# One group of a fused attention and feed-forward kernel: the output store, one second-layer product and the key loads change places

## The chip, the cores and the metric

The kernel runs on one core of a Trainium2 chip. The time is device microseconds of one execution; the kernel before took 1843.82 us in the median of three runs (1843.07, 1843.82 and 1850.48). The engines are TensorE (PE for its matmuls, PEld for its weight loads), VectorE (DVE), ScalarE (ACT), GpSimd (POOL) and SyncE (SP), which here does nothing but issue DMAs.

## The reference

Two functions follow each other. First, attention against keys pooled 4 by 4, whose keys and values are the same matrix; then a feed-forward layer whose hidden units pass a softmax-weighted linear unit and a layer norm.

```
kv_pool = kv.reshape(B, H//4, 4, W//4, 4, C).mean(axis=(2, 4))      # B = 4, H x W = 384 x 32, C = 128
k = v = kv_pool.reshape(B, -1, C) @ w_sr                            # 768 keys in a batch
s = (q @ k.T) / sqrt(C);  a = exp(s - max(s));  a /= sum(a) + 1e-9  # 12288 queries in a batch
x = (a @ v).reshape(B * 12288, 128)
h = x @ w_in                                                        # 128 -> 1024
sm = exp(h - max(h)) / sum;   solu = h * sm
ln = (solu - mean) / sqrt(var + 1e-6) * g_ln
out = ln @ w_out                                                    # 1024 -> 128
```

## The kernel before, in words

The 4 x 12288 queries are cut into 384 tiles of 128 tokens (`NT`). Four tiles make a group (`GT = 4`, 96 groups), 24 groups a batch. Products are taken to nearly float32 precision by splitting each operand into a high and a low float16 part and adding three products.

A tile passes these steps, each named by its tensors in the profile:

- `s` (L587, PE): six matmuls of the queries with the 768 keys. DVE takes the maximum (`nm`, L608), ACT the exponential (L609) and the high half (`phl`, L611), DVE the low half (`phl`, L619). SP then issues a DMA transpose of `phl` into the group's tile `pT` (L622).
- `xa` (L647, PE): when all four tiles of a group lie in `pT`, 18 matmuls with 512 columns make the attention output for the whole group. They are handed out over four slots as 5, 5, 4 and 4. ACT and DVE take them out as `xh` (L654) and `xl` (L659).
- `zz` (L674, POOL) and `rz` (L682, DVE): the group's softmax sums and their reciprocals.
- `h` (L700, PE): six matmuls into the 1024 hidden units, with `junkd` (L708, DVE, the maximum), `e` (L724, ACT, the exponential), `u` (L738, DVE), `junk` (L803, ACT, the variance) and the two halves `uhl` (L755 and L762, POOL). SP issues a DMA transpose of `uhl` into `uT` (L777).
- `o` (L828, PE): 24 matmuls of 128 columns from `uT`, about three slots after its transpose was issued. Once in a group DVE scales the four tiles' result into `ob` (L851), and SP stores it (L860).

The order is written by hand. The main loop has a pass for each *slot*, one tile entering in each, and the tiles before it stand at later steps: in slot n, PE computes `s` of tile n+1, `h` of tile n-9 (`LH = 10`) and `o` of tile n-14 (`LO = 14`), and DVE, ACT, POOL and SP get their instructions in the same pass. Every engine runs its instructions in that order; semaphores join them. A group's slots are counted here from first to fourth by the remainder of the slot by 4 (0, 1, 2, 3). So the fourth slot of a group issues the last transpose into its `pT`, and the `xa` that needs all four begins two slots later, in the second slot of the next group.

PSUM has three buffers that `s` and `h` take in turn (`ps_r`): an `h` can begin only when DVE has read the `s` of that slot for its `phl` (L619).

The keys of the next batch are made beside all this. Each of the 16 parts of the next `kv` is loaded with one DMA of 384 KB (`kv_load`, L227) and added up by POOL in two halves (`kv_add`, L238, tensor `ka`). `kv_plan` gives the slots: the load in the first slot of a group, the two additions three and five slots behind the slot that it is reckoned from. In the kernel before, ACT issues 42 of these loads, in between its own work. SP issues the transposes of `phl` and `uhl` in every slot, the store in the third slot, and the load of the queries (`q_load`, L528) in the fourth.

Of the kernel before, what the change touches and what calls it, by code (L numbers as in the profile page):

```python
# [30 lines left out]
NT = B * TPB  # L31
GT = 4
GPB = TPB // GT
NG = NT // GT
# [9 lines left out]
LO = 14  # L44
# [17 lines left out]
FIT_AT = 302  # L62

SOON = {0: (), 1: (8, 8), 2: (8, 8), 3: (27, 33), 4: (39, 45), 5: (51, 54)}
LATE = {6: (12, 16, 18), 7: (16, 20, 22)}


@with_exitstack
def kernel(
# [15 lines left out]
    nc = tc.nc  # L85
# [61 lines left out]
    state = {}  # L147

    def kv_alloc(b):
        for n, w, dt, bufs in (  # L150
            ("kT", NK, F32, 1),
            ("ksq", NK, BF16, 1),
            ("kss", 2, F32, 4),
            ("vf", NK, F32, 1),
        ):
            state[n, b] = bat.tile([P, w], dt, tag=n, name=f"{n}_{b}", bufs=bufs)
        for n, w in (("knm", 3), ("sv", 2), ("bb", 5), ("kq", 3), ("dg", P)):
            state[n, b] = (
                state[n, 0]
                if 0 < b < B  # L160
                else bat.tile([P, w], F32, tag=n, name=f"{n}_{b}", bufs=1)
            )
        for n, dt, bufs in (
            (("kwh", F32R, 1), ("kwl", F32R, 1))
            if b == 0 or b >= B
            else (("kh", F16, 2), ("kl", F16, 2))
        ):
            state[n, b] = bat.tile([P, NK], dt, tag=n, name=f"{n}_{b}", bufs=bufs)
        vhl = dmt.tile([P, 2 * NKC, P], F16, tag="vhl", name=f"vhl_{b}")
        state["vhl", b] = vhl  # L170
        state["vh", b], state["vl", b] = vhl[:, :NKC, :], vhl[:, NKC:, :]
# [327 lines left out]
    def kv_plan(b):  # L499


        for pos in range(RR):


            if b == 1 and pos in SOON:
                for half, slot in enumerate(SOON[pos]):
                    yield slot, [partial(kv_add, b, half, pos)]
                continue
            slot = 6 * pos - (28 if b == 1 else 30)
            load, *adds = (slot // GT * GT, slot + 3, slot + 5)  # L510
            if b == 1 and pos in LATE:
                load, *adds = LATE[pos]
            yield load, [partial(kv_load, b, pos)]
            if pos:
                for half, add in enumerate(adds):
                    yield add, [partial(kv_add, b, half, pos)]
        for slot, half, *fs in key_steps(b):
            yield slot, [partial(f, b, half) for f in fs]
# [18 lines left out]
    def wide(g):  # L537
        return g < GPB or g >= NG

    def q_scale(g):  # L540
        if wide(g) or NG <= g:
            return
        qf = state["qf", g // QL][:, (g % QL) * 512 : (g % QL + 1) * 512]
        nc.gpsimd.tensor_scalar(
            qf, qf, state["kq", g // GPB][:, 1:2], 1.0, op0=ALU.mult, op1=ALU.mult
        )
# [80 lines left out]
    def values(g, qtr, part):  # L627
        share = {0: [0, 9, 9, 0], 1: [0, 6, 6, 6]}.get(
            g, [4, 5, 5, 4] if wide(g + 2) else [5, 5, 4, 4]
        )  # L630
        s0 = sum(share[:qtr])
        s1 = s0 + share[qtr]
        if s0 == s1:
            return
        cut = s0 + (s0 > 0 and (qtr > 1 or wide(g + 2)))
        s0, s1 = ((s0, cut), (cut, s1))[part]
        b = g * GT // TPB
        if s0 == 0 and s1:
            state["xa", g] = ps_x.tile([P, 512], F32, tag="x", name=f"xa_{g}")
        if s0 == s1:  # L640
            return
        xa, pT = state["xa", g], state["pT", g]
        vh, vl = state["vh", b], state["vl", b]
        seq = [(a, c, v) for c in range(NKC) for (a, v) in ((0, vh), (1, vh), (0, vl))]
        for n in range(s0, s1):
            a, c, v = seq[n]
            nc.tensor.matmul(  # L647
                xa, v[:, c, :], pT[:, :, a * NKC + c, :], start=n == 0, stop=n == len(seq) - 1
            )
# [195 lines left out]
        nc.gpsimd.tensor_tensor(f, f2, state.pop(("v3", g)), op=ALU.add)  # L845
        nc.gpsimd.tensor_tensor(f2, f, mhalf[:, :GT], op=ALU.pow)

    def final_out(g, to=None):
        _, f = state["f", g]
        ob = dmt.tile([P, GT, P], F32, tag="ob", name=f"ob_{g}")  # L850
        nc.vector.scalar_tensor_tensor(  # L851
            ob,
            state["po", g].rearrange("p (j c) -> p j c", j=GT),
            swi,
            f.unsqueeze(2).to_broadcast([P, GT, P]),
            op0=ALU.mult,
            op1=ALU.mult,
        )
        rows = out[g * GT * P : (g + 1) * GT * P, :] if to is None else to
        nc.sync.dma_start(rows.rearrange("(p j) c -> p (j c)", j=GT), ob.rearrange("p j c -> p (j c)"))  # L860

# [174 lines left out]
    def key_steps(b):  # L1036
        steps = [
            (70, 0, kv_kp, kv_ko), (71, 1, kv_kp, kv_ko), (74, 2, kv_kp, kv_ko),
            (72, 0, kv_sq), (75, 1, kv_sq),
            (77, 0, kv_kh), (79, 1, kv_kh),  # L1040
            (78, 0, kv_kl), (80, 1, kv_kl),
        ]
        if b < B - 1:
            return steps + [
                (82, 0, kv_vp, kv_vo), (83, 1, kv_vp, kv_vo), (86, 2, kv_vp, kv_vo),
                (84, 0, kv_v_high), (85, 0, kv_v_low), (87, 1, kv_v_high), (88, 1, kv_v_low),
            ]
        return steps + [
            (82, 0, kv_v_scale), (84, 1, kv_v_scale),
            (83, 0, kv_vt_high), (86, 1, kv_vt_high),  # L1050
            (86, 0, kv_vt_low), (88, 1, kv_vt_low),
            (90, 0, kv_v_turn),
        ]
# [3 lines left out]
    def at(t, fn, *args):  # L1057
        if 0 <= t < NT:
            fn(t, *args)

    def at_last(t, fn, *args):

        if 0 <= t < NT and t % GT == GT - 1:
            fn(t // GT, *args)

    def at_soon(t, fn):

        at_last(t, fn) if t >= GT else fn(0) if t == GT - 2 else None
# [9 lines left out]
    for slot in range(NT):  # L1078
        i = slot - LH
        av, qtr = divmod(slot - LAV - GT + 1, GT)  # L1080
        tb, ti = divmod(slot, TPB)
        if ti == 12 and tb + 1 < B:
            kv_alloc(tb + 1)
        qs = GT if slot < 2 * GT else 2 * GT + 1 if slot < 3 * GT else 3 * GT + QSP
        todo = plan.pop(slot, [])
        at(slot, scores_exp)
        for f in held:
            f()
        held = []
        if slot <= LH:  # L1090
            at(slot - 1, scores_split)
        at(i - 1, hidden_u)
        at_last(slot - XSP - 1, values_split)
        if slot < 9:
            for f in fill.pop(slot, []):
                f()
        if 0 <= av < NG:
            values(av, qtr, 0)
        if slot != 8:
            at(slot + 2 if slot < 8 else slot + 1, scores_pe)  # L1100
        at_soon(slot - NORM, values_norm)
        at_last(slot - FSC, final_scale)
        at(i - 1, hidden_high)
        at(i - 1, hidden_low)
        at_last(slot - FSC, final_root)
        if slot < NT and 0 < qs < slot and (slot - 1 - qs) % GT == 0:
            q_low(slot // GT + 1)
        if slot < NT and 0 < qs <= slot + 1 and (slot + 1 - qs) % GT == 0:
            q_scale((slot + 1) // GT + 1)
        if slot < NT - 1:  # L1110
            at(i - 1, hidden_var)
        at(i, hidden_max)
        at(i, hidden_exp)
        if slot == NT - 1:
            hidden_var(i - 1)
        for f in fill.get(slot, []):
            f()
        pairs = [st for st in todo if len(st) > 1 and st[0].func is not kv_add]
        for st in pairs:
            st[0]()  # L1120
        if 0 <= av < NG:
            values(av, qtr, 1)
        for st in pairs:
            held += st[1:]
        if slot >= LH:
            at(slot, scores_split)
        at_soon(slot - NORM, values_recip)
        at_soon(slot - NORM, values_recip_u)
        at(i + 1, hidden_pe)
        if slot < NT - 1:  # L1130
            at(slot - LO, final_pe)
        at(i - 1, hidden_turn)
        if slot % GT == GT - 1:
            q_load(slot // GT + 3)
        at_last(slot - LO - 1, final_out)
        at_last(slot - XSP, values_out)
        for st in todo:
            if st[0].func is kv_add:
                for f in st:
                    f()  # L1140
            elif len(st) == 1:
                st[0]()
        if slot < NT and 0 < qs <= slot and (slot - qs) % GT == 0:
            q_split(slot // GT + 1)
# [183 lines left out]
```

## Time and profile before

| | |
|---|---|
| median of three runs | 1843.82 us |
| the profiled execution | 1843.65 us |
| its span, first to last instruction | 1841.9 us |
| PE, DVE, ACT, POOL busy | 99%, 96%, 95%, 91% of the span |
| DMA transposes, `phl` and `uhl` | 384 and 383 |
| key loads issued by ACT and by SP | 42 and 22 |
| mean DMA rate over the span | 235 GB/s |

The share of busy time says little here, as four engines are nearly full. A wait between two of them and the time from one group to the next say more. The group's period is read as the time between the same instruction of two groups, here DVE's `u` (L738) of one tile in four.

### The profile page before, as it was taken

The numbers are of one execution on the slowest core, as the hardware profiler recorded it, in microseconds if no ns is written. First come the engines' busy times: TensorE is split into PE (matmuls) and PEld (weight loads), VectorE is DVE, ScalarE is ACT, GpSimd is POOL, SyncE is SP. The second block draws the span as 40 slices with busy tenths as digits, with TensorE's granted clock in tenths as the row PEclk, the third lists the DMA queues.
The fourth block names the chain that finished last, engine by engine and source line by source line (L and its number), as shares of the span: only waits on it lengthen the run. The fifth ranks groups of instructions, "written<-read, shape, count | busy, mean of one in ns | idle before, by whom it ended". The sixth has DMA issues, their size and how long they took to land.

```text
span 1841.9 us, 42770 instructions
## 1 busy us (share of the span) xinstructions
PE 1818.3 (99%) x15747; PEld 1218.5 (66%) x15747; DVE 1761.9 (96%) x2635; ACT 1742.6 (95%) x3129; POOL 1667.2 (91%) x1466
## 2 busy tenths in 40 slices
PE   8999999999999999999999999999999999999998
PEld 5577777777666666666666666666666666666666
DVE  6999999999999999999999998999999999999997
ACT  5999999999999999999999998999999999999997
POOL 5899999899999999989999998998988988888887
PEclk9999999999999999999999999999999999999999
DMA  9999999999999999999999999999999999999997
GB/s 301 203 249 230 230 253 232 247 230 237 242 241 241 246 245 242 246 235 235 247 239 241 242 222 230 247 239 224 222 233 230 232 235 231 220 235 224 230 223 168
DMA packets 1440027, 432.80 MB, mean 235 GB/s; under 512 B 1404608, under 2 KB 1408832, under 8 KB 1439552
## 3 DMA queue, kind: packets, MB, share of 16 engines
q1 hardware_dynamic: 1433616, 413.45, 112.6%
q10 hardware_dynamic: 6192, 16.52, 3.2%
q8 instruction: 126, 2.06, 0.5%
q14 instruction: 93, 0.76, 0.1%
HBM read 52.50 MB, written 25.17 MB: 42 GB/s over the span
## 4 chain that ended last, share of the span: by engine, by line
PE 46%; DVE 26%; ACT 15%; issue 9%; DMA 2%; POOL 1%; SPq 0%; DVEq 0%; ACTq 0%; POOLq 0%
PE o L828 13%; PE h L700 13%; PE s L587 10%; PE xa L647 10%; DVE junkd L708 8%; DVE phl L619 6%; DVE nm L608 5%; ACT e L724 4%; ACT junk L803 4%; DVE u L738 3%; ACT phl L611 3%; ACT s L609 2%; DVE ob L851 2%; DVE xl L659 2%; DMA kv<-in_kv_dram 1%
## 5 line engine op out<-in xcount | busy, mean ns | idle before, releaser
L762 POOL TENSOR_TENSOR uhl<-u,uhl 128x1024 f16<-128x1024 f32 x382 | 815.0, 2134 | 32.3 <-ACT uhl L753 0.6
L828 PEld LDWEIGHTS <-uT 128*128 128x128 f16 x9072 | 537.9, 98 | 89.1 <-issue 0.9
L828 PE MATMUL o<-wch,uT 128*128 128x128 f16 x6048 | 568.1, 219 | 0.1
L828 PE MATMUL o<-wcl,uT 128*128 128x128 f16 x3024 | 526.1, 219 | 0.0
L738 DVE SCALAR_TENSOR_TENSOR u<-h,rz,e 128x1024 f32<-128x1024 f32 x384 | 490.4, 1277 | 33.3 <-ACT e L724 32.7
L708 DVE TENSOR_SCALAR_CACHE_REDUCE junkd<-h,rz 128x1024 bf16<-128x1024 f32 x384 | 490.7, 1278 | 7.6 <-PE h L700 7.2
L647 PE MATMUL xa<-pT,vhl 128*128 128x512 f16 x1728 | 470.4, 380 | 5.4 <-DMA pT<-phl 5.4
L755 POOL TENSOR_SCALAR uhl<-u 128x1024 f16<-128x1024 f32 x379 | 395.8, 1044 | 83.9 <-DVE u L738 72.7
L724 ACT ACTIVATE e<-h,nm,rz 128x1024 f32<-128x1024 f32 x384 | 458.5, 1194 | 8.2 <-DVE junkd L708 8.2
L803 ACT ACTIVATE junk<-u,su 128x1024 bf16<-128x1024 f32 x384 | 438.0, 1141 | 0.1
L609 ACT ACTIVATE s<-s,nm 128x768 f32<-128x768 f32 x384 | 334.7, 872 | 47.6 <-DVE nm L608 47.1
L619 DVE SCALAR_TENSOR_TENSOR phl<-s,phl 128x768 f16<-128x768 f32 x384 | 365.8, 953 | 6.5 <-ACT phl L611 4.1
L608 DVE TENSOR_REDUCE nm<-s 128x1 f32<-128x768 f32 x384 | 360.1, 938 | 9.1 <-PE s L587 4.6
L611 ACT ACTIVATE phl<-s 128x768 f16<-128x768 f32 x384 | 311.1, 810 | 12.1
L700 PEld LDWEIGHTS <-xh 128*128 128x128 f16 x1536 | 144.0, 97 | 195.4 <-issue 27.1
L647 PEld LDWEIGHTS <-vhl 128*128 128x128 f16 x1728 | 162.4, 98 | 141.3 <-issue 16.0
L700 PE MATMUL h<-w_in_h,xh 128*128 128x512 f16 x768 | 228.9, 380 | 3.6 <-DVE rz L682 3.2
L700 PE MATMUL h<-w_in_l,xh 128*128 128x512 f16 x768 | 229.0, 380 | 0.0
L700 PE MATMUL h<-w_in_h,xl 128*128 128x512 f16 x768 | 228.8, 380 | 0.0
L587 PEld LDWEIGHTS <-qh 128*128 128x128 f16 x1152 | 122.6, 114 | 42.9
L587 PE MATMUL s<-kh,ql 128*128 128x384 f16 x576 | 140.8, 326 | 0.1
L587 PE MATMUL s<-kl,qh 128*128 128x384 f16 x576 | 140.8, 326 | 0.0
(153 smaller groups left out, 1820.4 us busy)
## 6 DMA issues: line engine op xcount, KB each, us to landing
qf<-in_q_dram SPq DMA_DIRECT2D x96, 256.0 KB, 3.8
out_dram<-ob SPq DMA_DIRECT2D x96, 256.0 KB, 2.9
kv<-in_kv_dram ACTq DMA_DIRECT2D x42, 384.0 KB, 4.3
kv<-in_kv_dram SPq DMA_DIRECT2D x22, 384.0 KB, 7.5
pT<-phl SPq DMA_TRANSPOSE x384, 4.0
uT<-uhl SPq DMA_TRANSPOSE x378, 4.6
raw_in<-in_moe_w_in_dram SPq DMA_DIRECT2D x1, 1024.0 KB, 5.1
raw_out<-in_moe_w_out_dram SPq DMA_DIRECT2D x1, 1024.0 KB, 9.6
```

Of the source, the lines that this page charges most:

```text
L587: nc.tensor.matmul(s[:, half, :384], tokens(lh)[:, j, :], rh[:, half * 384 : (half + 1) * 384], start=n == 0, stop=n == 2,)
L608: nc.vector.tensor_reduce(nm, s, axis=AX.XY, op=ALU.max, negate=True)
L619: nc.vector.scalar_tensor_tensor(phl[:, 1], state.pop(("s", t)), SC, phl[:, 0], op0=ALU.mult, op1=ALU.subtract)
L647: nc.tensor.matmul(xa, v[:, c, :], pT[:, :, a * NKC + c, :], start=n == 0, stop=n == len(seq) - 1)
L700: nc.tensor.matmul(h[:, hs], lh[:, ts], rh[:, hs], start=n == 0, stop=n == 2)
L708: nc.vector.tensor_scalar(junk, state["h", t], state["rz", g][1][:, j : j + 1], None, op0=ALU.mult, op1=ALU.min, accum_out=nm,)
L724: nc.scalar.activation(e, state["h", t], AF.Exp, bias=nm, scale=state["rz", g][0][:, js], accum_out=state["z2", g][:, js],)
L738: nc.vector.scalar_tensor_tensor(u, state.pop(("h", t)), state["rz", g][2][:, j : j + 1], state.pop(("e", t)), op0=ALU.mult, op1=ALU.mult, ...
L755: nc.gpsimd.tensor_scalar(uhl[:, 0, :], u, 1.0, 1.0, op0=ALU.mult, op1=ALU.mult)
L762: low.tensor_tensor(uhl[:, 1, :], u, uhl[:, 0, :], op=ALU.subtract)
L803: nc.scalar.activation(junk, u, AF.Square, scale=-float(DFF), bias=su, accum_out=state["v3", g][:, j : j + 1],)
L828: nc.tensor.matmul(po[:, ts], uT[:, a * NFC + c, :], w[:, c, :], start=start, stop=stop)
```

## The change

Three pieces of the order move; nothing is added or left out in the computation.

- *The store.* DVE's `ob` stays in the third slot, but its store is issued in the fourth, behind that slot's two transposes and ahead of the load of the queries.
- *The second slot's matmuls.* In the second slot of a group PE runs `o`, then `h`, then `xa`, where it ran `xa`, `h`, `o`.
- *The key loads.* The 42 loads that ACT issued are issued by SP, one slot later, in a group's second slot behind its two transposes. The additions keep their slots.

```diff
-LATE = {6: (12, 16, 18), 7: (16, 20, 22)}
+LATE = {6: (13, 16, 18), 7: (17, 20, 22)}
...
             slot = 6 * pos - (28 if b == 1 else 30)
-            load, *adds = (slot // GT * GT, slot + 3, slot + 5)
+            load, *adds = (slot // GT * GT + 1, slot + 3, slot + 5)
...
-            yield load, [partial(kv_load, b, pos)]
+            yield load, [partial(kv_load, b, pos, nc.sync)]
...
-    def final_out(g, to=None):
+    def final_out(g, to=None, later=False):
...
+        state["ob", g] = ob
+        if not later:
+            final_store(g, to)
+
+    def final_store(g, to=None):
+        ob = state.pop(("ob", g))
         rows = out[g * GT * P : (g + 1) * GT * P, :] if to is None else to
         nc.sync.dma_start(rows.rearrange("(p j) c -> p (j c)", j=GT), ob.rearrange("p j c -> p (j c)"))
...
-        if 0 <= av < NG:
+        o_first = slot % GT == 1
+        if o_first:
+            at(slot - LO, final_pe)
+        elif 0 <= av < NG:
             values(av, qtr, 1)
...
         at(i + 1, hidden_pe)
-        if slot < NT - 1:
+        if o_first:
+            if 0 <= av < NG:
+                values(av, qtr, 1)
+        elif slot < NT - 1:
             at(slot - LO, final_pe)
         at(i - 1, hidden_turn)
+        at_last(slot - LO - 2, final_store)
         if slot % GT == GT - 1:
             q_load(slot // GT + 3)
-        at_last(slot - LO - 1, final_out)
+        at_last(slot - LO - 1, partial(final_out, later=True))
```

SP's instructions from the second slot of a group to the first of the next, with a key load in the group. The first number behind a name is the tile's or the group's (`phl_193` is of tile 193, in slot 193; `ob_44` is of group 44). Before:

```order
L622 DMA_TRANSPOSE pT_48_13759<-phl_193_13803 128x12x128
L777 DMA_TRANSPOSE uT_182_13873<-uhl_182_13820 128x16x128
L622 DMA_TRANSPOSE pT_48_13759<-phl_194_13881 128x12x128
L777 DMA_TRANSPOSE uT_183_13943<-uhl_183_13893 128x16x128
L860 DMA out_0_dram<-ob_44_13945 128x512
L622 DMA_TRANSPOSE pT_48_13759<-phl_195_13951 128x12x128
L777 DMA_TRANSPOSE uT_184_14015<-uhl_184_13967 128x16x128
L528 DMA qf_51_14017<-in_q_dram 128x512
L622 DMA_TRANSPOSE pT_49_14050<-phl_196_14023 128x12x128
```

The same stretch of SP now:

```order
L622 DMA_TRANSPOSE pT_48_13759<-phl_193_13801 128x12x128
L777 DMA_TRANSPOSE uT_182_13871<-uhl_182_13818 128x16x128
L227 DMA kv_3_5_13873<-in_kv_dram 128x768
L622 DMA_TRANSPOSE pT_48_13759<-phl_194_13881 128x12x128
L777 DMA_TRANSPOSE uT_183_13943<-uhl_183_13893 128x16x128
L622 DMA_TRANSPOSE pT_48_13759<-phl_195_13950 128x12x128
L777 DMA_TRANSPOSE uT_184_14014<-uhl_184_13966 128x16x128
L866 DMA out_0_dram<-ob_44_13945 128x512
L528 DMA qf_51_14017<-in_q_dram 128x512
L622 DMA_TRANSPOSE pT_49_14050<-phl_196_14023 128x12x128
```

The store is no longer ahead of the last transpose into `pT_48` (that of `phl_195`), and the key load is there, behind `uT_182`. On ACT this load stood between the group's `xh` and the exponential of `s_193`, before:

```order
L803 ACTIVATE junk_181_13749,v3_45_13549<-u_181_13734,su_181_13735 128x1024
L724 ACTIVATE e_182_13754,z2_45_13548<-h_182_13693,nm2_182_13751,rz_45_13525 128x1024
L654 ACTIVATE xh_46_13795<-xa_46_13538,sv_0_115 128x512
L227 DMA kv_3_5_13798<-in_kv_dram 128x768
L609 ACTIVATE s_193_13738,z_all_80<-s_193_13738,nm_193_13800 128x2x384
L611 ACTIVATE phl_193_13803<-s_193_13738 128x768
```

There it is gone, and the rest of ACT keeps its order, as do DVE and POOL. PE in the second slot (slot 193), from its last `s` to its last kind of work; lines that repeat a kind are left out. Before:

```order
L587 MATMUL s_194_13809<-kh_2_7595,ql_48_13585 128x384
...
L647 MATMUL xa_47_13830<-pT_47_13469,vhl_1_641 128x512
...
L700 MATMUL h_184_13842<-w_in_h_94,xh_46_13795 128x512
...
L828 MATMUL o_44_13627<-wch_96,uT_179_13652 128x128
...
L587 MATMUL s_195_13886<-kh_2_7595,qh_48_13584 128x384
```

And now:

```order
L587 MATMUL s_194_13807<-kh_2_7595,ql_48_13585 128x384
...
L828 MATMUL o_44_13627<-wch_96,uT_179_13652 128x128
...
L700 MATMUL h_184_13858<-w_in_h_94,xh_46_13795 128x512
...
L647 MATMUL xa_47_13865<-pT_47_13469,vhl_1_641 128x512
...
L587 MATMUL s_195_13886<-kh_2_7595,qh_48_13584 128x384
```

`xa` and `o` have changed places around `h`; in the other three slots PE's order is the same.

## Rows read from the trace of the kernel before

**Rows 1.** Waits over the span: engine, line, waited for: us, times, longest

```profile
DVE u L738 <- ACT e L724: 32.7, 94, 0.7
...
PE xa L647 <- DMA pT<-phl: 5.4, 2, 2.7
...
PE h L700 <- DVE rz L682: 3.2, 8, 0.6
```

**Rows 2.** Timeline, a group around 920 us: start, us, engine, line, operation [idle <-releaser]

```profile
918.45 0.88 ACT L609 ACTIVATE s<-s,nm 128x768 f32<-128x768 f32 x1 [0.56 <-DVE nm L608]
...
922.91 1.28 DVE L738 SCALAR_TENSOR_TENSOR u<-h,rz,e 128x1024 f32<-128x1024 f32 x1 [0.35 <-ACT e L724]
```

**Rows 3.** Timeline of DVE, one `u` in each of four successive groups

```profile
1092.52 1.28 DVE L738 SCALAR_TENSOR_TENSOR u<-h,rz,e 128x1024 f32<-128x1024 f32 x1
...
1113.57 1.27 DVE L738 SCALAR_TENSOR_TENSOR u<-h,rz,e 128x1024 f32<-128x1024 f32 x1
...
1131.95 1.28 DVE L738 SCALAR_TENSOR_TENSOR u<-h,rz,e 128x1024 f32<-128x1024 f32 x1
...
1154.78 1.27 DVE L738 SCALAR_TENSOR_TENSOR u<-h,rz,e 128x1024 f32<-128x1024 f32 x1
```

**Rows 4.** Timeline around the first long group, SP, ACT's queue and PE

```profile
1090.62 0.53 SPq L860 DMA_DIRECT2D out_dram<-ob  x1
...
1091.24 1.74 SPq L622 DMA_TRANSPOSE pT<-phl  x1
...
1092.14 0.33 ACTq L227 DMA_DIRECT2D kv<-in_kv_dram  x1
...
1094.57 0.49 PE L587 MATMUL s<-kh,qh 128*128 128x384 f16 x2
...
1098.43 1.24 PE L647 MATMUL xa<-pT,vhl 128*128 128x512 f16 x5 [2.72 <-DMA pT<-phl]
```

**Rows 5.** Timeline around the second long group

```profile
1130.85 1.66 SPq L622 DMA_TRANSPOSE pT<-phl  x1
...
1131.67 0.34 ACTq L227 DMA_DIRECT2D kv<-in_kv_dram  x1
...
1137.94 1.91 PE L647 MATMUL xa<-pT,vhl 128*128 128x512 f16 x5 [2.70 <-DMA pT<-phl]
```

**Rows 6.** Timeline, PE and DVE in the second slot of an ordinary group

```profile
910.82 0.49 PE L587 MATMUL s<-kh,qh 128*128 128x384 f16 x2
...
911.74 0.95 DVE L619 SCALAR_TENSOR_TENSOR phl<-s,phl 128x768 f16<-128x768 f32 x1
...
911.79 1.24 PE L647 MATMUL xa<-pT,vhl 128*128 128x512 f16 x5
...
912.87 0.59 PE L700 MATMUL h<-w_in_h,xh 128*128 128x512 f16 x2
...
914.17 0.22 PE L828 MATMUL o<-wch,uT 128*128 128x128 f16 x1
...
914.74 1.28 DVE L708 TENSOR_SCALAR_CACHE_REDUCE junkd<-h,rz 128x1024 bf16<-128x1024 f32 x1
...
915.51 0.49 PE L587 MATMUL s<-kh,qh 128*128 128x384 f16 x2
```

**Rows 7.** DMA issues: tensor, queue, count, KB each, median us to landing

```profile
kv<-in_kv_dram ACTq DMA_DIRECT2D x42, 384.0 KB, 4.3
kv<-in_kv_dram SPq DMA_DIRECT2D x22, 384.0 KB, 7.5
```

**Rows 8.** Timelines of SP, POOL and DVE from one group's second slot on

```profile
1026.42 3.24 SPq L777 DMA_TRANSPOSE uT<-uhl  x1
...
1034.51 1.00 POOL L238 TENSOR_TENSOR ka<-ka,kv 128x384 f32<-128x384 f32 x1
...
1039.53 0.61 POOL L674 TENSOR_SCALAR zz<-z_all,bb 128x4 f32<-128x4 f32 x2
...
1041.31 0.19 DVE L682 RECIPROCAL rz<-zz 128x8 f32<-128x8 f32 x1
```

## The prediction

> **What bounds the kernel now.** Four engines are busy for over nine tenths of the span, so I read the waits between them first, then one group in order of time, then the time from group to group.
>
> The waits show a ring of two engines. DVE's `u` waits for ACT's `e` 94 times in 96 groups, 0.35 us each [rows 1]. The timeline of an ordinary group shows the other half: in its third slot ACT waits 0.56 us for DVE's maximum before it can start the exponential of `s`, then runs its queue without a pause up to `e`, and DVE's `u` starts only when that is done [rows 2]. Between its `u` of one group and the maximum of the next DVE has no pause either. A ring in which each engine in turn waits for the other sets a period by itself: 1113.57 to 1131.95, 18.38 us [rows 3]. PE is no part of that ring.
>
> PE's own work in a group is nearly as long. In the second slot `s` takes 0.97 us (910.82 to 911.79), five matmuls of `xa` 1.08, `h` 1.30 and `o` 1.34 [rows 6]. Four times `s`, `h` and `o` and 18 times 0.216 for `xa` make 14.44 + 3.89 = 18.33 us. So PE has 0.05 us of air in a group, and takes it in the second slot, where `h` begins 0.18 us behind the end of DVE's `phl` (911.74 + 0.95 = 912.69), which frees its PSUM buffer.
>
> The groups that don't keep the period come next. Two stand out: 1092.52 to 1113.57 is 21.05 us, and 1131.95 to 1154.78 is 22.83 [rows 3], 2.66 and 4.44 too long, 7.10 us together. In both PE stands before `xa` in the second slot and waits 2.7 us for the transposes into `pT` [rows 4, 5]; these are the only two waits of this kind in the span [rows 1]. In the second one the matmuls behind the wait run slowly as well, 1.91 us for five where the first has 1.24.
>
> Why there? The fourth slot's transpose was issued at 1091.24 and was needed at 1094.57 + 0.97 = 1095.54. SP was late: the store had just been issued at 1090.62, and 0.90 us behind the transpose ACT issued a key load of 384 KB [rows 4]. In the second case the load follows the transpose by 0.82 us [rows 5]. So in both, the one transpose that PE waits for shared the DMA engines with a key load, in the first with the store as well.
>
> **The change part by part.**
>
> *o ahead of h and xa.* `xa` begins behind `o` and `h`, 1.34 + 1.30 = 2.64 us later in its slot. The wait at 1098.43 is 2.89 us against 1095.54, so 0.25 is left. The wait for `pT` can't reach DVE's ring any more by that piece alone.
>
> *The store behind the transposes.* The transpose into `pT` no longer queues behind the store on SP. Where SP is late, that is 1091.24 − 1090.62 = 0.62 us earlier, more than the 0.25 left. The queries' load and the next slot's transpose come as much later; that `pT` is first read more than four slots on, and the queries are loaded for a group two further on, so I count nothing. `ob` is ready a slot earlier than before relative to its store, so SP waits less there.
>
> *The key load on SP, a slot later.* It no longer meets the fourth slot's transpose. ACT loses 42 issues, which cost its datapath nothing today, as they sit in its queue beside running work. SP gains 42 issues of 0.33 us [rows 4], 13.9 us in all. Where SP has a pause before the next `phl` is ready, it covers them; where it has none, the third slot's transposes come 0.33 us later, and none of these is the last of its `pT`. I take 0; the bounds are 0 and 13.9.
>
> The Trainium skill speaks against this part ("DMA: Bandwidth & Descriptors", section "Queues, rings and completion order"): each DMA engine takes turns between the queues that have work, packet by packet, and consumes one queue's descriptors in order. By that rule a load on ACT's queue overtakes transposes that SP has already queued, which fits the slow transposes of rows 4 and 5, and a load on SP's queue lands only behind them. What this would cost is the third rival.
>
> *What the keys' additions need.* 20 of the 42 loads (those whose additions begin in the group's fourth slot) have the first addition only two slots behind. The tightest ordinary case: SP is through with the second slot's `uT` at 1026.42 + 3.24 = 1029.66, and POOL adds at 1034.51, so the load has 4.85 us to land [rows 8]. A load from ACT lands in 4.3 us in the median, one of the 22 of the start, issued in a burst on SP, in 7.5 [rows 7]. If POOL waits, its `zz` comes later; it ends at 1040.14 and DVE needs it at 1041.31, so 1.17 us more is free [rows 8]. I take 4.3 to 6.0 us, which costs nothing, since the new place is no burst but one load between transposes.
>
> *h later.* In the second slot `h` starts behind `s` and `o`, at 910.82 + 0.97 + 1.34 = 913.13 instead of 912.87, 0.26 later. It no longer waits for `phl`. It leaves PE at 914.43 instead of 914.17, and DVE takes it up at 914.74 behind other work [rows 6]; 0.31 of 0.57 us is left. So DVE's ring should not feel it, and the ordinary group keeps its 18.38 us: the 0.05 us of air only moves to another slot.
>
> *The groups in which keys are made.* There PE has more to do, and eight times `h` waits for DVE up to 0.6 us, 3.2 us in all [rows 1] (`rz` is the last step that DVE has done then). With `o` ahead each such wait is 0.26 us shorter, 8 x 0.26 = 2.1 at most. PE and the ring take turns as the bound there, so I take half, 1.0; bounds 0 and 3.2.
>
> Sum: the profiled execution took 1843.65 us, its span 1841.9 and 1.75 around it. 1843.65 − 7.1 − 1.0 = 1835.5. The median of the runs is 0.17 above the profiled one, so 1835.7.
>
> **The rivals.**
>
> *PE is the ring after all.* If PE's second slot paces the ordinary group too, its wait there goes as well: 18.38 − 18.33 = 0.05 us in some 70 groups, 3.5 us, and with the whole 3.2 of the key groups 1843.8 − 7.1 − 3.2 − 3.5 = 1830. For it: PE is the fullest engine. Against: rows 2 close without PE.
>
> *The late transposes only move.* Both long groups arose because SP was behind. PE's wait also let SP catch up. Without that, with 0.33 us more for each key load, SP could stay late until `uT` or a `pT` holds PE elsewhere. Then the 7.1 us come back in other groups: 1843. For it: in the stretch of rows 4 SP goes from issue to issue. Against: `o` has slots of room for its `uT`, and `xa` has 2.64 us more.
>
> *Slower: key loads land late.* On SP's queue a load stands behind the second slot's `uT`, itself just issued. If it lands in 7.5 us as the early loads do [rows 7], POOL's addition waits 7.5 − 4.85 = 2.65 us, `zz` comes as much later, and DVE, which takes its instructions in order, stands before `rz` for 2.65 − 1.17 = 1.48 us with its maximum and `u` queued behind it. That is in the ring. Twenty times it is 30 us at this tightest room; where the room is 1.5 us larger nothing is lost, so about half, 15 us: 1843.8 − 8.1 + 15 = 1851, at worst 1866. It decides from 4.85 + 1.17 = 6.0 us to landing. For it: 7.5. Against: 4.3, and that the 7.5 come from a queue of 22 loads.
>
> **How the numbers follow.** The forecast, that both waits go and nothing takes their place, gets 0.58, with a range of 1832 to 1840; PE as the ring 0.12; the late transposes that move 0.20; the late key loads 0.10. A measurement of this kernel can tell about 0.5% from no change, 9.2 us: faster is below 1834.6, slower above 1853.0. The forecast stands 1.1 us on the near side of that line, and a third of its range is beyond it: 0.58 / 3 = 0.19, with 0.11 of the PE rival 0.30. Slower gets half of the last rival and a little, 0.06. The rest, 0.64, is the same. The range goes from the PE rival, 1830, to just over the case in which the waits move, 1845.
>
> **What would show it.** Right: no wait of `xa` for `pT` in the view of waits; the group period still 18.38, with DVE's `u` still waiting for `e`; the two long groups gone; key loads from SP landing in under 6 us; PE's small wait in another slot than the second. The store's step would be wrong if the fourth slot's transposes were issued as late as before. Waits of POOL's `ka` for `kv`, and of DVE's `rz` for `zz`, would show the third rival; waits of `o` for `uT`, or of `xa` in groups that had none, the second; a period under 18.38 the first.

## The result and the profile after

| | before | changed |
|---|---|---|
| median of five runs each, side by side | 1843.82 us | 1862.93 us |
| lowest and highest | 1841.04, 1850.48 | 1859.97, 1866.29 |
| the profiled execution, its span | 1843.65, 1841.9 | 1866.29, 1864.5 |

The changed kernel is slower: the ratio is 1.0094, 95% interval 1.0071 to 1.0116. Its profiled execution is the slowest of its five. The forecast was 1835.7 us with 1830 to 1845. The time lies 18 us above the range, and near the rival of the late key loads (1851, at worst 1866).

The view of waits of the changed kernel (engine, line, waited for: us, times, longest):

```profile
DVE u L738 <- ACT e L724: 32.7, 91, 0.8
POOL ka L238 <- DMA kv<-in_kv_dram: 31.3, 17, 3.0
...
DVE rz L682 <- POOL zz L674: 14.2, 14, 2.3
ACT phl L611 <- DMA pT<-phl: 12.8, 15, 2.5
PE o L828 <- DMA uT<-uhl: 10.6, 10, 2.2
...
PE h L700 <- DVE rz L682: 1.8, 3, 1.4
...
PE xa L647 <- DMA pT<-phl: 0.2, 1, 0.2
```

Against [rows 1]: the ring of `u` and `e` is as it was, and `xa`'s 5.4 us have shrunk to 0.2. Four waits are new, all of them for DMAs or behind one.

Where the 22.6 us of span went is read from one instruction, DVE's `phl` of the first tile of groups 21, 46, 68 and 94. Timeline of the kernel before:

```profile
404.90 0.95 DVE L619 SCALAR_TENSOR_TENSOR phl<-s,phl 128x768 f16<-128x768 f32 x1
...
869.97 0.95 DVE L619 SCALAR_TENSOR_TENSOR phl<-s,phl 128x768 f16<-128x768 f32 x1
...
1283.88 0.95 DVE L619 SCALAR_TENSOR_TENSOR phl<-s,phl 128x768 f16<-128x768 f32 x1
...
1762.50 0.95 DVE L619 SCALAR_TENSOR_TENSOR phl<-s,phl 128x768 f16<-128x768 f32 x1
```

And of the changed kernel:

```profile
412.70 0.95 DVE L619 SCALAR_TENSOR_TENSOR phl<-s,phl 128x768 f16<-128x768 f32 x1
...
889.96 0.95 DVE L619 SCALAR_TENSOR_TENSOR phl<-s,phl 128x768 f16<-128x768 f32 x1
...
1306.80 0.96 DVE L619 SCALAR_TENSOR_TENSOR phl<-s,phl 128x768 f16<-128x768 f32 x1
...
1785.47 0.95 DVE L619 SCALAR_TENSOR_TENSOR phl<-s,phl 128x768 f16<-128x768 f32 x1
```

The distance is 7.80, 19.99, 22.92 and 22.97 us. The 42 later key loads are issued in groups 3 to 63: the loss builds up where keys are loaded, and behind that both kernels run alike, 18.38 us a group.

One long group of the changed kernel shows the new waits at work (timeline of SP, POOL, PE and DVE; the group's `u` at 891.69 and the next at 913.01 are 21.32 us apart):

```profile
880.30 0.95 DVE L619 SCALAR_TENSOR_TENSOR phl<-s,phl 128x768 f16<-128x768 f32 x1
...
881.82 1.42 SPq L622 DMA_TRANSPOSE pT<-phl  x1
883.33 3.78 SPq L777 DMA_TRANSPOSE uT<-uhl  x1
887.16 0.58 SPq L227 DMA_DIRECT2D kv<-in_kv_dram  x1
887.84 1.50 SPq L622 DMA_TRANSPOSE pT<-phl  x1
...
891.93 1.00 POOL L238 TENSOR_TENSOR ka<-ka,kv 128x384 f32<-128x384 f32 x1 [1.48 <-DMA kv<-in_kv_dram]
...
896.03 0.23 PE L828 MATMUL o<-wch,uT 128*128 128x128 f16 x1 [1.14 <-DMA uT<-uhl]
...
897.80 0.61 POOL L674 TENSOR_SCALAR zz<-z_all,bb 128x4 f32<-128x4 f32 x2
...
898.44 0.20 DVE L682 RECIPROCAL rz<-zz 128x8 f32<-128x8 f32 x1 [2.29 <-POOL zz L674]
```

SP issued the key load at 887.16, behind two transposes of 1.42 and 3.78 us, and POOL wanted it at 891.93 − 1.48 = 890.45. Its addition, and then `zz`, came late, and DVE stood 2.29 us before `rz` with its maximum and `u` behind it. At 896.03 PE's `o` waited 1.14 us for a `uT` as well. SP itself is late: the `pT` of 887.84 is the transpose of the `phl` that DVE finished at 880.30 + 0.95 = 881.25, 6.59 us before.

This *lag* (from the end of DVE's `phl` to the issue of its transpose) is the number to follow. Averaged over the tiles of groups 21 to 63 it is 1.87 us in the kernel before and 5.72 in the changed one; in groups 68 to 90, without key loads, 0.48 and 0.82.

The key loads themselves land as fast as forecast (DMA issues of the changed kernel: tensor, queue, count, KB each, median us to landing):

```profile
kv<-in_kv_dram SPq DMA_DIRECT2D x64, 384.0 KB, 4.5
...
pT<-phl SPq DMA_TRANSPOSE x384, 4.3
uT<-uhl SPq DMA_TRANSPOSE x378, 4.7
```

The 4.5 us are of all 64; the 42 later ones alone land in 4.2. They are late because they are issued late.

### The profile page after: what moved, and what is told of

It is laid out like the page before. It is cut to its first block, busy times and chain, and to the rows that moved or that the text cites. A ratio compares the mean times of both kernels' runs of the same rounds, so it can differ in the third digit from the quotient of the medians.

```text
span 1864.5 us, 42727 instructions
## 1 busy us (share of the span) xinstructions
PE 1826.3 (98%) x15747; PEld 1222.0 (66%) x15747; DVE 1767.8 (95%) x2635; ACT 1745.1 (94%) x3129; POOL 1668.1 (89%) x1466
## 4 chain that ended last, share of the span: by engine, by line
PE 42%; POOL 27%; DVE 9%; issue 9%; ACT 9%; DMA 3%; POOLq 0%; SPq 0%; DVEq 0%; ACTq 0%
PE o L828 12%; PE h L700 12%; POOL uhl L762 11%; PE s L587 8%; PE xa L647 8%; POOL uhl L755 7%; POOL ka L238 3%; DVE junkd L708 2%; DVE phl L619 2%; ACT e L724 2%; ACT junk L803 2%; ACT phl L611 2%; DVE nm L608 2%; POOL ql L574 2%; POOL f L846 2%
## 5 line engine op out<-in xcount | busy, mean ns | idle before, releaser
L828 PE MATMUL o<-wch,uT 128*128 128x128 f16 x6048 | 570.0, 219 | 11.0 <-DMA uT<-uhl 10.6
L611 ACT ACTIVATE phl<-s 128x768 f16<-128x768 f32 x384 | 311.1, 810 | 24.8 <-DMA pT<-phl 12.8
L587 PE MATMUL s<-kh,qh 128*128 128x384 f16 x576 | 140.9, 326 | 3.7 <-DVE u L738 3.5
```

What stands on the lines that cost most here:

```text
L587: nc.tensor.matmul(s[:, half, :384], tokens(lh)[:, j, :], rh[:, half * 384 : (half + 1) * 384], start=n == 0, stop=n == 2,)
L828: nc.tensor.matmul(po[:, ts], uT[:, a * NFC + c, :], w[:, c, :], start=start, stop=stop)
```

## The experiments

In all of them the kernel before ran beside the others; its medians in the five sets were 1844.29 (e1 to e4), 1844.16 (e5 to e8), 1845.19 (e9 to e12), 1845.61 (e13 to e16) and 1848.34 (e17, e18). "Lag" is the one just defined, of the profiled execution.

| | median, us | ratio to before, 95% | lag, us |
|---|---|---|---|
| e1 keys back on ACT | 1864.65 | 1.0100 (1.0072 to 1.0129) | 5.4 |
| e2 keys on SP alone | 1857.49 | 1.0077 (1.0057 to 1.0097) | 3.7 |
| e3 keys a group earlier | 1854.46 | 1.0067 (1.0044 to 1.0089) | 6.0 |
| e4 o ahead alone | 1854.32 | 1.0058 (1.0037 to 1.0079) | 5.6 |
| e5 o ahead, few keys | 1837.58 | 0.9958 (0.9934 to 0.9982) | 0.7 |
| e6 4 KB loads on SP | 1872.61 | 1.0147 (1.0109 to 1.0185) | 4.2 |
| e7 store, queries on ACT | 1878.12 | 1.0183 (1.0146 to 1.0220) | 2.0 |
| e8 the same, of changed | 1870.76 | 1.0152 (1.0113 to 1.0192) | 4.8 |
| e9 before again | 1845.08, one run | | 2.4 |
| e10 o ahead again | 1851.79, one run | | 5.2 |
| e11 store alone | 1856.00 | 1.0054 (1.0030 to 1.0079) | 3.3 |
| e12 keys in halves | 1845.87 | 1.0006 (0.9986 to 1.0026) | 2.2 |
| e13 a kick | 1850.13 | 1.0040 (1.0016 to 1.0064) | 2.4 |
| e14 three loads out | 1851.71 | 1.0023 (0.9998 to 1.0048) | 5.1 |
| e15 4 KB loads on ACT | 1849.46 | 1.0021 (0.9995 to 1.0048) | 2.7 |
| e16 o ahead late | 1843.83 | 0.9989 (0.9963 to 1.0015) | 2.8 |
| e17 changed, few keys | 1836.12 | 0.9950 (0.9932 to 0.9967) | 1.3 |
| e18 before, few keys | 1838.78 | 0.9960 (0.9945 to 0.9974) | 0.8 |

### The change piece by piece: e1 to e4, e11

**e1**: the changed kernel, keys back on ACT in the first slot.

```diff
-LATE = {6: (13, 16, 18), 7: (17, 20, 22)}
+LATE = {6: (12, 16, 18), 7: (16, 20, 22)}
...
-            load, *adds = (slot // GT * GT + 1, slot + 3, slot + 5)
+            load, *adds = (slot // GT * GT, slot + 3, slot + 5)
...
-            yield load, [partial(kv_load, b, pos, nc.sync)]
+            yield load, [partial(kv_load, b, pos)]
```

> The changed kernel with its key loads back on ACT in a group's first slot; the store and o ahead stay as changed. Theory A (late landing: SP issues the key loads late, POOL's additions wait for them, zz and with it DVE's rz come late): all of the 19 us are the key loads', so 1834 to 1840, with no wait of ka for kv and none of xa for pT. Theory B (overload: with the key loads in it SP's one queue has more to issue than fits in a group, and everything on it runs late): the same 1834 to 1840, and SP's transposes issued about 2 us behind their halves as in the kernel before, not 5. Theory C (o ahead itself costs, as it takes 2.4 us from the room of the uT that it reads): still over 1850, with o waiting for uT.

**e2**: the kernel before, only the keys moved to SP and the second slot (the first three pieces of the diff).

> The kernel before with nothing but the key loads moved to SP and to the second slot. Theories A and B: about 1860 to 1870, as in the changed kernel or a little more, since the two long waits of xa for pT can stay or multiply when SP is late (B: several more of them, as the fourth slot's transpose is late in every group with a key load). Theory C: within 5 us of the kernel before.

**e3**: the changed kernel, each key load a group earlier on SP.

```diff
-            yield load, [partial(kv_load, b, pos, nc.sync)]
+            yield load - (0 if b == 1 and pos in (13, 14) else 4), [partial(kv_load, b, pos, nc.sync)]
```

> The changed kernel with each key load issued by SP one group (four slots) earlier, except two that have no free buffer then; the additions keep their slots. Theory A: POOL no longer waits, DVE's rz neither, so all of the loss goes: 1834 to 1842. Theory B: POOL's waits go, but SP issues as much in a group as before, so its transposes stay 4 to 6 us late and PE waits for uT, ACT for pT, in more places: 1850 to 1865.

**e4**: the kernel before, only `o` ahead (the pieces with `o_first`).

> The kernel before with o ahead of h and xa in the second slot and nothing else. Theories A and B: the two waits of xa for pT go and nothing comes for them, 1835 to 1840. Theory C: o waits for uT in the second slot, 1850 or more.

**e11**: the kernel before, only the store later (`final_store`).

> The kernel before with the store alone moved behind the fourth slot's transposes. Theory D: the same issues and bytes, only 0.6 us are moved from ahead of the last pT of a group to behind it, so xa's wait has 0.6 us more room and the drift stays: 1840 to 1846. By the prediction's step for the store (it frees xa's transpose): 1838 to 1842. If later stores hurt (they then stand beside the load of the queries, in a burst of 512 KB ahead of the next group's transposes): the lag climbs as with o ahead, 1850 to 1860.

Each of the three pieces alone is slower than before, by 10 to 13 us, and all three together by 19: they don't add. In e1 and e3 POOL's additions wait nowhere for `kv`, and the loss stays (e1) or halves (e3). So the chain from `ka` to `rz`, seen so plainly in the long group, isn't what the loss hangs on; where it is taken away, other waits hold the late transposes up. The view of waits of e4, which has SP's order unchanged:

```profile
ACT phl L611 <- DMA pT<-phl: 15.5, 15, 3.5
PE xa L647 <- DMA pT<-phl: 13.7, 11, 3.7
...
PE o L828 <- DMA uT<-uhl: 1.2, 2, 0.7
```

With 2.64 us more room `xa` waits 11 times where it waited twice. The transposes had become later by more than the room: the lag went from 1.9 to 5.6 us. Theories A (a late landing) and B (the keys on SP's one queue) fell here as sole causes; C (o ahead costs by its place) stood.

### Without the key loads: e5, e17, e18

**e5** is e4, **e17** the changed kernel and **e18** the kernel before, each without 32 of its 42 later key loads (the diff is against e4 and the kernel before; in e17 the load that stays has `nc.sync`). The additions take the part loaded last, so POOL's work stays and the sums are others.

```diff
-            yield load, [partial(kv_load, b, pos)]
+            if pos % 4 == 0:
+                yield load, [partial(kv_load, b, pos)]
...
-        nc.gpsimd.tensor_tensor(ka, x, state["kv", b, pos][:, half, :], op=ALU.add)
+        part = pos if ("kv", b, pos) in state else pos // 4 * 4
+        nc.gpsimd.tensor_tensor(ka, x, state["kv", b, part][:, half, :], op=ALU.add)
```

> The kernel before with o ahead in the second slot, and with 32 of the 42 key loads on ACT's queue left out: the additions take the part loaded last instead, so the sums are other numbers and POOL's work is the same. Theory D (SP's one stream of issues and the DMA engines behind it are full wherever keys are loaded, so that any lateness stays and grows until some wait stops it): without these 12 MB the lag of the transposes stays under 2 us, the waits of ACT's phl for pT (15.5 us with all loads) and of xa for pT (13.7) go to nearly nothing, and the time is 1833 to 1840. Theory C (o ahead costs by its place on PE, as it takes room from o for its uT or moves h): the waits and the time stay where they were with all loads, 1850 to 1858.

> The changed kernel with 32 of its 42 key loads on SP left out, the additions take the part loaded last. Theory D (with the key loads the transposes have no time to spare, and any order that makes them later pays in stops): the lag stays near 1 us, no waits of ka for kv, of o for uT or of phl for pT, 1835 to 1840, all runs within 3 us of each other. Rival: the new order of store and matmuls costs by itself (the version with o ahead ran 1837.6 without these loads, so then it is the store): 1845 or more.

> The kernel before with the same 32 loads left out. Theory D: both long groups go, 1836 to 1840, all runs within 3 us of each other; against the changed kernel without them the difference is what the change is worth without the crowd, 1 to 2 us by the prediction's step for the groups in which keys are made. Rival, that the scatter of the kernel before has another cause than key loads: 1837 to 1856 as with all loads.

All three fall to 1836 to 1839, and no wait for `pT`, `uT` or `kv` in the main loop is left. The runs draw together, too: 1838.29 to 1839.52 in twelve runs of e18, where the kernel before went from 1836.81 to 1856.82 in the second set. So key loads make both the loss and the scatter, and theory C falls: `o` in its new place costs nothing by itself. Side by side without this crowd of loads the changed kernel is 1838.78 − 1836.12 = 2.7 us *faster*.

### What is short, SP's time or the DMA engines'? e6, e15, e7, e8, e12

Where keys are loaded SP has hardly a pause. Its instructions in the kernel before (timeline), each some 0.1 us behind the end of the one before:

```profile
537.47 0.57 SPq L528 DMA_DIRECT2D qf<-in_q_dram  x1
538.15 2.30 SPq L622 DMA_TRANSPOSE pT<-phl  x1
540.54 2.13 SPq L777 DMA_TRANSPOSE uT<-uhl  x1
542.76 1.60 SPq L622 DMA_TRANSPOSE pT<-phl  x1
```

Summed over groups 21 to 63 the issues take 17.55 us of an 18.68 us group, and the 0.1 us between its ten or eleven instructions nearly all the rest; pauses over 0.2 us come to 8.0 us in the 800 us from 440 to 1240, and to 2.4 in the changed kernel. Without 32 of the key loads (e18), which are ACT's and not SP's, SP's issues take 16.89 us of an 18.52 us group and the pauses come to 30.9 us: the transposes themselves are issued faster then.

**e6** puts one more load on SP in each group with a key load, of 4 KB, and **e15** the same on ACT:

```diff
+    def extra(b, pos):
+        e = dmt.tile([P, NFC], F32, tag="ex", name=f"ex_{b}_{pos}", bufs=4)
+        nc.sync.dma_start(e, g_ln)
...
             yield load, [partial(kv_load, b, pos)]
+            yield load + 1, [partial(extra, b, pos)]
```

> The kernel before as it is, and one more load of 4 KB on SP in the second slot of each group that has a key load: it takes SP's time for an issue and hardly any of the DMA engines'. Theory D in its form that SP's own time is short: SP has some 0.1 us of pause in such a group, the issue takes 0.3 to 0.6, 42 of them 13 to 24 us, so 1852 to 1866, with late pT or uT in the waits, as with the key loads alone on SP (1857). Theory D in its form that only the bytes count: 4 KB are nothing, 1842 to 1846. Theory A (only a late key load costs): no change either, since the keys are loaded by ACT as before.

> The kernel before with the 42 extra loads of 4 KB on ACT's queue instead of SP's. If SP's own time for an issue is what costs (28 us for 42 of them on SP): 1842 to 1847. If the work of any load, however small, is what costs: 1865 to 1875.

On SP the 42 loads cost 1872.61 − 1844.16 = 28.5 us. One is issued in 0.57 us (timeline of e6):

```profile
532.07 0.57 SPq L234 DMA_DIRECT2D ex<-in_moe_g_ln_dram  x1
```

With 0.1 us behind it, 42 × 0.67 = 28.1, within the interval of the measurement (20 to 34 us): in this stretch an issue on SP costs about its full time. On ACT the same loads make no difference that can be told, 1.0021 (0.9995 to 1.0048).

**e7** goes the other way. It is e11 with the store and the queries on ACT's queue; **e8** does that to the changed kernel.

```diff
-        nc.sync.dma_start(t, qT[b, :, gb * 512 : (gb + QL) * 512])
+        nc.scalar.dma_start(t, qT[b, :, gb * 512 : (gb + QL) * 512])
...
-        nc.sync.dma_start(rows.rearrange("(p j) c -> p (j c)", j=GT), ob.rearrange("p j c -> p (j c)"))
+        nc.scalar.dma_start(rows.rearrange("(p j) c -> p (j c)", j=GT), ob.rearrange("p j c -> p (j c)"))
```

> The kernel before with the store a slot later and on ACT's queue, and the load of the queries on ACT's queue: SP is left with the transposes and loses 0.55 + 0.58 = 1.1 us of issues in a group, the bytes stay. Theory D with SP's time as the short thing: the transposes' lag falls under 1 us, both long groups go, 1833 to 1839. With the bytes as the short thing: the lag stays near 2 us, 1841 to 1848. A rival: the two issues take ACT's time, and ACT is in the ring that sets the period: 2 x 0.33 us in 96 groups are 63 us, 1900.

> The changed kernel with its store and its load of the queries on ACT's queue, keys on SP: SP loses 0.58 + 0.44 = 1.0 us of issues in a group against the changed kernel and is then 0.7 us under the kernel before. Theory D with SP's time as the short thing: lag under 2 us, no waits of ka for kv, of rz for zz or of o for uT, 1833 to 1842. With the bytes as the short thing: 1855 to 1866 as the changed kernel. Theory A (a key load that stands behind two transposes in one queue is late for its addition): ka still waits for kv some 17 times, 1855 to 1866.

Both are slower than with all on SP, which neither form of theory D expected. The rival that the two issues take ACT's time isn't borne out: in groups 68 to 90, where no keys are loaded, e7 has them on ACT as well and takes 405.16 us against 405.08. SP loses 1.1 us of issues in a group of e7, and gets little of it back: over groups 21 to 63 the issue of a `uT` takes 2.78 us in the mean instead of 2.52, that of a `pT` 1.69 instead of 1.60, together 1.4 us a group (four of each). Landing takes longer too (DMA issues of e7; before it was 4.0 and 4.6 for `pT` and `uT`):

```profile
pT<-phl SPq DMA_TRANSPOSE x384, 4.4
uT<-uhl SPq DMA_TRANSPOSE x378, 5.1
```

So the time of a transpose on SP isn't SP's own: it is longer when other queues move more meanwhile. Taking loads off ACT's queue shows the same: in e18 the two are 2.40 and 1.53. The Trainium skill ("Perfetto Trace Analysis", section "DMA Instruction — HWDGE (DVE, Sync)") has the reported span of such an instruction last until all its descriptors are made; the rows of e7 agree as far as they show that span growing when another queue is loaded. Both things are short at once: an issue that moves almost nothing takes SP's time from the transposes (e6), and bytes on another queue go with longer ones (e7, e18). That this makes up all of the 34 us of e7 is not shown: its mean lag is 2.0 us, no more than before.

**e12** cuts each key load on ACT in two halves, two slots apart.

> The kernel before with each key load on ACT's queue as two of 192 KB, the second two slots later: the same bytes in smaller bursts. If the lag jumps because a burst of 384 KB stops the transposes at once: no stops of xa left, 1836 to 1841. If only the sum of the bytes counts: 1842 to 1848. If each load's own cost counts (as 42 loads of 4 KB on SP cost 28 us): slower, 1855 to 1872.

As before, 1.0006 (0.9986 to 1.0026): a second issue on ACT costs nothing that can be told, and smaller bursts gain nothing, which speaks for the sum of the bytes. The one profile is of a faster run (1841.12 us) and has no wait of `xa` for `pT` over 0.5 us, the sign of the burst theory, so that theory is weakened and not excluded.

### Does lateness come by chance, and does it stay? e9, e10, e13, e14, e16

**e9** and **e10** are second profiles of the kernel before and of e4. **e13** delays SP once, with two loads of 256 KB, in group 27 of the kernel before. **e14** is e4 without the key loads of groups 22, 24 and 25. **e16** is e4 with `o` ahead only from group 57 on, where the kernel before had its two long groups.

```diff
+    def kick():
+        for n in range(2):
+            k = dmt.tile([P, 512], F32, tag="kick", name=f"kick_{n}", bufs=1)
+            nc.sync.dma_start(k, qT[0, :, n * 512 : n * 512 + 512])
+
+    plan.setdefault(109, []).append([partial(kick)])
```

```diff
-        o_first = slot % GT == 1
+        o_first = slot % GT == 1 and slot >= 228
```

> The kernel before, unchanged, a second profile of it. Theory D (with key loads the DMA engines need about as much time as a group lasts, so the transposes' lag drifts until a wait stops it): the lag climbs somewhere else than in the first profile (there from group 57 on, two stops of xa at groups 58 and 60), with 1 to 4 stops of xa for pT of up to 2.8 us, span 1837 to 1852. A rival, that the two long groups come from their place in the order: the same two stops again, at the same two groups.

> The kernel before with o ahead in the second slot, a second profile of it. If o ahead changes the drift itself and not only luck: the lag climbs past 4 us early again (in the first profile at group 25) and stays at 5 to 7 until the key loads end, span 1847 to 1858. If it was luck: the lag stays under 2.5 us for most of the key loads, span 1837 to 1845.

> The kernel before with two loads of 256 KB more on SP, one behind the other, once, in the second slot of group 27: SP is then some 4 us later. Theory E (two states: lateness of 5 us keeps itself up, as the loads of other engines then meet other transposes): the lag goes from 1.7 to 5 there and stays at 4 to 7 until the key loads end at group 63, 1850 to 1860. Theory F (the drift of the kernel before is small by itself, and o ahead makes it larger): the lag returns to 1.5 to 2 within ten groups, 1842 to 1848.

> The kernel before with o ahead, and three key loads (groups 22, 24 and 25) left out, their additions take the part before: the lag, 2.2 us at group 24 and 6.6 at group 28 with all loads, should be under 1 us at group 26. Theory E: it then stays under 2.5 us like that of the kernel before, up to group 57 at least, 1838 to 1846. Theory F: it climbs past 4 us again within ten to fifteen groups, 1847 to 1857.

> The kernel before with o ahead only from group 57 on, where its two long groups are: if the prediction's step holds in that place (xa gets 2.4 us more, and both stops go), 1836 to 1840. If the lag climbs to the next wait there as in the version with o ahead everywhere (at group 63 a stop of 5 us): 1842 to 1848.

e9 had long groups at the same two places as the first profile (groups 58 and 60), as the rival said and theory D did not, and a third at 41. But the profile of e16, whose order is that of the kernel before up to group 57, has its stops earlier (timeline of PE):

```profile
468.28 1.25 PE L647 MATMUL xa<-pT,vhl 128*128 128x512 f16 x5 [1.19 <-DMA pT<-phl]
...
713.29 1.24 PE L647 MATMUL xa<-pT,vhl 128*128 128x512 f16 x5 [2.26 <-DMA pT<-phl]
...
733.25 1.25 PE L647 MATMUL xa<-pT,vhl 128*128 128x512 f16 x5 [1.48 <-DMA pT<-phl]
...
1056.73 1.69 PE L647 MATMUL xa<-pT,vhl 128*128 128x512 f16 x5 [2.69 <-DMA pT<-phl]
```

So the same instructions run into lateness in one execution and not in another, and the two long groups weren't a fixed place that an edit could mend. From group 57 on, with `o` ahead, e16 had no long group and a lag of 1.5 us, as the prediction's step has it; in the median it gained nothing, 0.9989 (0.9963 to 1.0015).

In the profile of e13 the delay led to three stops of `xa` within fifteen groups and was then gone, the lag back at 1.6: in this run lateness doesn't keep itself up in the kernel before. But it is the fastest of ten (1846.78 us), and four of the others took 1858, as theory E had it, with a median of 1850.13; so theory E isn't excluded. e14 shows the opposite with `o` ahead. Timeline of DVE and SP, two tiles and their transposes:

```profile
512.53 0.95 DVE L621 SCALAR_TENSOR_TENSOR phl<-s,phl 128x768 f16<-128x768 f32 x1
513.50 1.41 SPq L624 DMA_TRANSPOSE pT<-phl  x1
...
540.30 0.95 DVE L621 SCALAR_TENSOR_TENSOR phl<-s,phl 128x768 f16<-128x768 f32 x1
...
546.99 1.42 SPq L624 DMA_TRANSPOSE pT<-phl  x1
```

The transpose is issued 0.02 us behind its tile at 513.50, and 5.74 us behind it at 546.99, with two key loads in between; from then on the lag stays at 4 to 8 until they end. In the kernel before the same two key loads leave it at 1.5. So theory F, that `o` ahead makes the drift larger, is borne out from group 22 on, in both profiles of e4 and here, but not everywhere: e16 shows seven groups without it, and from group 5 to 21, where keys are loaded too and most groups take 18.73 us, e4 needs 302.65 us and the kernel before 302.71. *Why* isn't settled either: SP's order, its issues and the bytes are the same. What differs over groups 21 to 63 is 0.4 us a group in the length of the transposes' issues (`uT` 2.61 us in the mean, `pT` 1.62).

## Why the prediction was wrong

**The step that failed** is that "both waits go and nothing takes their place". It rests on three parts, each put at a gain or at nothing, and each alone made the kernel slower: `o` ahead by 10.0 us (e4), the store by 10.8 (e11), the key loads on SP by 13.2 (e2). All three count on time to spare for the transposes, on SP and in the DMA engines behind it, and where keys are loaded there is next to none; without those loads the same change gains 2.7 us (e17 against e18).

**The key loads on SP**: "SP gains 42 issues of 0.33 us ... I take 0; the bounds are 0 and 13.9". The 0.33 us were ACT's [rows 4]; SP takes 0.57 and 0.1 more until the next. And "where SP has a pause ... it covers them": SP has hardly any where keys are loaded. e6 priced 42 issues at 28.5 us, twice the upper bound; the move itself costs 13.2 (e2), near the bound and not 0, and why it costs less than e6 is not shown. The rows to see it were there: I wrote that SP "goes from issue to issue" in the stretch of rows 4, counted it for a rival only, and never summed SP's issues over a group as I did for PE. This part alone is not the cause, though: with the keys back on ACT the loss is as large (e1).

**`o` ahead.** That `pT` "can't reach DVE's ring any more by that piece alone" was wrong: in e4 `xa` waits 11 times, 13.7 us. In the changed kernel `xa`'s wait went, but its cause, transposes that run late, stayed and came out at the next waits: `o` for `uT` 10.6 us, ACT's `phl` for `pT` 12.8. The rival *the late transposes only move* had this mechanism. It priced it at the 7.1 us given back, and the lag grew instead, from 1.9 to 5.7 us.

**The store.** I expected the last `pT` 0.62 us earlier and counted nothing for what comes later. Alone it costs 0.54% (e11), with a lag of 3.3 us. SP has the same issues, and only their order changed; by what way that makes the transposes later is open, as for `o`.

**The key loads' landing**, 4.3 to 6.0 us forecast, was 4.2, no later than on ACT's queue (4.3). The rival of late key loads had the right chain and even its price (15 us for DVE's waits before `rz`, measured 14.2), for another reason: not a landing over 6.0 us but an issue 5 us late. And e1 shows that without that chain the time is the same. A chain that is plain in the profile needn't be the cause.

**Right, and small:** the ordinary group keeps 18.38 us. `h`'s wait for `rz` fell from 3.2 to 1.8 us, where I counted 1.0 as gained.

No version with all its key loads beats the kernel before; e12, e15 and e16 can't be told from it. In the set of e18, 32 of its key loads, had they been free, were worth 1848.34 − 1838.78 = 9.6 us in the medians.

## What to carry to other kernels

Sum the issues of a DMA queue over one period, pauses between them included, as you would an engine's work: a queue that fills the period is a bound, though no view of busy time lists it, and here each issue added to it cost about its full time (e6). A wait that disappears only moves if what made it late is still full; look for what is full before counting the wait as gain. And test a chain by taking it away before calling it the cause.

## What the hardware showed

*Transposes stop beside an instruction fetch.* Four microseconds of DMA traffic of the kernel before, 40 slices of 0.1 us, and the queue of instructions in them:

```profile
GB/s 238 279 287 292 274 236 187 228 218 279 272 272 277 228 417 236 38 26 0 0 0 0 0 0 0 0 8 8 8 10 10 8 10 10 218 297 292 287 287 289
...
q8 instruction: 1, 0.02, 1.9%
```

For some 1.7 us nearly nothing moves while one packet of 16 KB of instructions comes in. The page of the kernel before lists 126 such packets, one in 14.6 us. Around the 86 of them from 450 to 1700 us the transposes' packets fall, in the median, from some 540 in half a microsecond to 13, and are back 2 us behind the start of the fetch. That is about a tenth of the time. That the fetch is the cause is inferred from this regular meeting. In e4 and e14 these fetches meet other transposes than in the kernel before (at 514.6, 529.7 and 545.0 us in e4, at 517.7, 533.7 and 548.3 before), which may be how a mere order on PE changes the transposes' length; it was not tried.

*Behind a stop of PE the clock can be lower.* The second long group of the kernel before (windows; PE busy is the first column behind the length, PEclk the third from the end):

```profile
1134.00:1138.00 4.00, 1.30 (x12) 0.73 (x10) 4.00 (x6) 4.00 (x9) 3.66 (x4) 1.00 1.22 207
1138.00:1142.00 4.00, 4.00 (x11) 1.42 (x12) 0.10 (x2) 1.95 (x4) 3.77 (x4) 0.57 1.22 252
1142.00:1146.00 4.00, 4.00 (x39) 2.78 (x38) 3.79 (x6) 1.37 (x3) 0.56 (x1) 1.00 1.15 255
```

Behind a stop of 2.7 us the granted clock is at 1.2 GHz for 3.41 us, which is 1.7 us of work lost. That is about the difference between the two long groups, 2.66 and 4.44 us, which the prediction had left as matmuls that "run slowly": the first had a stop as long and no such stretch. The changed kernel has two such stretches in its main loop, at 338 and 683 us, at the ends of stops of 2.15 and 1.98 us, and one at its start.
